# A fourth row buffer and one more unit of lead in a fused attention and gated-layer kernel

## The chip, the cores and the metric

The kernel runs on one core of a Trainium2 chip. The metric is the device time of one execution in microseconds (us); the number given for the kernel before is the median of three runs. Engines are named as in the profile: PE is TensorE (PEld its weight loads), DVE is VectorE, ACT is ScalarE, POOL is GpSimd and SP is SyncE, which does no arithmetic and here issues most of the transfers.

## The reference

Talking-heads attention feeds a gated layer. With batch 4, 12 heads, 448 positions and head size 64, all in float32:

```python
scores = scale * np.matmul(q, k.transpose(0, 1, 3, 2))
scores = np.einsum('bhij,hg->bgij', scores, w_pre)      # first mix over the heads
scores = scores - np.max(scores, axis=-1, keepdims=True)
attn = np.exp(scores)
attn = attn / (np.sum(attn, axis=-1, keepdims=True) + 1e-09)
attn = np.einsum('bhij,hg->bgij', attn, w_post)         # second mix over the heads
attn_out = np.matmul(attn, v)
x = attn_out.transpose(0, 2, 1, 3).reshape(1792, 768)
gate = 1.0 / (1.0 + np.exp(-(x @ w_gate)))
return (gate * (x @ w_val)) @ w_out                     # 768 -> 1536 -> 768
```

## The kernel before

The first 400 us are the attention, the rest is the gated layer, whose matrix products go by a scheme with seven products in place of eight and whose tasks are ordered by a planner with fixed costs. The planner's list is cut at slots of the attention, and neither its costs nor its slots are touched by the change.

**Blocks and units.** Each of the four batches is cut into three blocks of 120 query rows and one of 88. A set is ten query rows with all twelve heads, 120 rows of scores. A unit is two sets; a block of 120 rows has six units, the last block of a batch four and one with a single set, so there are 23 units in a batch and 92 in all. Scores are computed on 128 positions at a time; the eight (or four) left over of each such piece are gathered for the last two units of a batch: the last but one uses a buffer of its own, `T_rest`, the last one, with the single set, an ordinary row buffer, filled by four small transfers.

**The way of a unit.** `scores` (L174) multiplies q with k; `keep` (L182, L185) copies the result from the banks into a stage `st`, half by ACT and half by DVE. `regroup` moves the rows of a unit from the stage into a row buffer `T`, where the 120 partitions are rows and heads, by two transfers on SP's queue (L238; L229 for the rest rows). `premix` (L257) does the first mix on PE from T into three banks `pm`. `rowmax` (L262, DVE), `expo` (L269, ACT), `norm` and `scale` (L274, L275, L281, POOL and DVE) and `p_lo` (L287, DVE) make the normalised weights in two halves; `postmix` (L299) does the second mix on PE, `mix` (L307, ACT) copies it out, and `av` (L326) multiplies a finished block with v. ACT copies that out (L336), and `flush` (L315) stores it through SP's queue.

**The order.** A loop over slots `s` writes the program; slot s has the second mix of unit s. Within it SP first gets the stores that the slot before left (`flush`), then the row transfers of unit s + LEAD (`rows_until`, `regroup`), with LEAD = 5; PE gets the first mix of unit s + 3 (SOFT), then a job of scores, then the second mix of unit s, then `av`. So a unit's rows are requested two slots before the slot of its first mix. The row buffers are used in turn, `t_bufs[u % len(t_bufs)]`: with three of them, the transfer for unit u overwrites what the first mix of unit u - 3 read, in the slot before. A table `plan` gives slots to the score jobs of the next block (from `first[bi - 1] - LEAD` to `first[bi] - LEAD`), to the loads of k (L147), q (L154) and v (L192), and to the early loads of the gated layer's weights (`raws`, L1088); all but the v and the weight loads depend on LEAD. SP takes its instructions in order: a transfer that waits holds all behind it. Before the first unit the loop runs LEAD slots in which only rows, scores and first mixes stand.

Of the kernel before, what the change touches and what calls it, by code (L numbers as in the profile page):

```python
# [9 lines left out]
F32 = mybir.dt.float32  # L10
# [39 lines left out]
def _attention(ctx, tc, ins, B, H, S, D, xs, raws, make_moe):  # L50
# [18 lines left out]
    tp, ep, pp, sm = (grp_ctx.enter_context(tc.tile_pool(name=f"a_{n}", bufs=b))  # L69
                          for n, b in (("t", 1), ("e", 3), ("p", 2), ("s", 4)))  # L70
# [89 lines left out]
    def jobs_of(bi):  # L160
        return NP * blocks[bi][6] // SB
# [48 lines left out]
    nm_t, e_t, ss_t, p_t, mx_t = {}, {}, {}, {}, {}  # L210
    mixes = [mp.tile([128, 4, H, QB], F32, name=f"mix{i}") for i in range(2)]

    t_bufs = [tp.tile([128, 2, S], F32, name=f"T{i}") for i in range(3)]
    t_rest = tp.tile([128, 2, S], F32, name="T_rest")
    for T in t_bufs + [t_rest]:
        nc.gpsimd.memset(T[:64 - HK], 0.0)
# [96 lines left out]
    def flush():  # L313
        while stores:
            nc.sync.dma_start(out=stores[0][0], in_=stores.pop(0)[1])  # L315
# [23 lines left out]
                flush()  # L339


    LEAD = 5
    SOFT = 3
    EARLY_AT = (5, 12, 19, 27, 34, 42, 49, 57)
    BOUND = (0, 6, 10, 11, 12, 13, 14)
# [2 lines left out]
    def at(slot, fn, *args):  # L348
        plan.setdefault(slot, []).append((fn, args))

    def spread(i, n, s0, s1):
        return s0 + i * (s1 - s0) // n

    taken = {EARLY_AT[k] + slot for k in range(moe.EARLY) for slot in (11, 12)}
    for b in range(B):
        f = first[PB * b]
# [13 lines left out]
        for c in range(NP if b else 0):  # L370
            at(spread(c, NP, first[PB * (b - 1)] + 6, first[PB * b - 1] - LEAD - 2), k_load, b, c)
    for bi in range(1, NBK):
        s0, s1 = first[bi - 1] - LEAD, first[bi] - LEAD
        n, skip = jobs_of(bi), 0
        if bi % PB == 0:
            s0, skip = first[bi - 2] - LEAD, jobs_of(bi - 1)
        elif n < NP and bi + 1 < NBK:
            s1 = first[bi + 1] - LEAD
        of = n + skip if skip else n + NP if n < NP and bi + 1 < NBK else n
# [68 lines left out]
    def rows_until(u, done):  # L448
        while done < min(NU, u + 1):
            regroup(done)  # L450
            done += 1
        return done

    next_dma = 0
    for s in range(min(min(plan), -LEAD), max(plan) + 1):
        flush()
        next_dma = rows_until(s + LEAD, next_dma)
        todo = plan.get(s, ())
# [798 lines left out]
@with_exitstack  # L1257
def kernel(ctx, tc, B, H, S, D, ins, out):
    nc = tc.nc
    top = ctx.enter_context(tc.tile_pool(name="top", bufs=1))  # L1260
    dram = ctx.enter_context(tc.tile_pool(name="dram", bufs=1, space=DRAM))
    xs = dram.tile([B, H * D // 128, 128, S], F32, name="xs")
    with tc.manual_schedule():
        raws = top.tile([128, 13 * H * D // 2], F32, name="raws")
        with ExitStack() as c2:
            moe = _attention(c2, tc, ins, B, H, S, D, xs, raws,
                             lambda NG: _Moe(tc, xs, ins, out, raws, NG, top))
        moe.run()
# [72 lines left out]
```

## Time and profile before

| | us |
|---|---|
| median of 3 runs (lowest, highest) | 843.75 (842.42, 844.67) |
| the profiled execution | 844.52 |
| its span | 842.7 |
| PE busy | 793.8 (94%) |
| DVE, ACT, POOL busy | 633.7, 563.7, 280.6 |
| granted PE clock, mean over the span | 0.975 |

The span runs from the first instruction of the profile to the last, and the execution's own time is 1.8 us longer. Busy times are those of instructions in work; a busy PE is not PE at its peak. In the slices of the page PE is at 9 tenths or more almost everywhere after 400 us and between 7 and 9 before; transfers have their densest slices at 6 to 8 tenths in the attention and at 9 late in the gated layer.

### The profile page before, as it was taken

The numbers are of one execution on the slowest core, as the hardware profiler recorded it, in microseconds if no ns is written. First come the engines' busy times: TensorE is split into PE (matmuls) and PEld (weight loads), VectorE is DVE, ScalarE is ACT, GpSimd is POOL, SyncE is SP. The second block draws the span as 40 slices with busy tenths as digits, with TensorE's granted clock in tenths as the row PEclk, the third lists the DMA queues.
The fourth block names the chain that finished last, engine by engine and source line by source line (L and its number), as shares of the span: only waits on it lengthen the run. The fifth ranks groups of instructions, "written<-read, shape, count | busy, mean of one in ns | idle before, by whom it ended". The sixth has DMA issues, their size and how long they took to land.

```text
span 842.7 us, 23449 instructions
## 1 busy us (share of the span) xinstructions
PE 793.8 (94%) x9530; PEld 432.9 (51%) x9530; DVE 633.7 (75%) x1068; ACT 563.7 (67%) x1106; POOL 280.6 (33%) x462
## 2 busy tenths in 40 slices
PE   8989799898989989896999989999999999999998
PEld 2446465464555555465555445555555555555554
DVE  4978587784887778778899799669986999998000
ACT  3888577884878877876777586657874776553100
POOL 1527456474456553342021331223322231110000
PEclk9999899997999999997999999999999999999999
DMA  5686458863786547455653453675546897987001
GB/s 193 214 235 197 149 149 234 260 185 103 227 235 208 163 159 222 156 169 172 218 169 121 151 176 146 229 244 188 174 161 219 313 344 314 340 333 284 34 29 71
DMA packets 80760, 166.13 MB, mean 197 GB/s; under 512 B 20492, under 2 KB 58220, under 8 KB 80652
## 3 DMA queue, kind: packets, MB, share of 16 engines
q1 hardware_dynamic: 72348, 132.83, 50.0%
q0 software_dynamic: 7728, 31.27, 9.4%
q8 instruction: 75, 1.23, 0.6%
q10 hardware_dynamic: 576, 0.53, 0.2%
q14 instruction: 33, 0.27, 0.1%
HBM read 87.75 MB, written 38.15 MB: 149 GB/s over the span
## 4 chain that ended last, share of the span: by engine, by line
PE 71%; DMA 17%; DVE 4%; ACT 4%; issue 1%; POOL 1%; SPq 1%; ACTq 0%; POOLq 0%; DVEq 0%
PE bank L1198 29%; PE bank L1209 17%; DMA T<-st 13%; PE pm L257 9%; PE qk L174 5%; PE av L326 5%; PE mx L299 5%; DMA k<-in_kp_dram 2%; DVE m L1182 1%; DMA v<-in_vb_dram 1%; ACT e L269 1%; DMA m<-w 1%; ACT raws L1129 1%; ACT mix L307 1%; POOL raws L1135 1%
## 5 line engine op out<-in xcount | busy, mean ns | idle before, releaser
L1198 PE MATMUL bank<-m,m 128*128 128x448 f16 x1152 | 221.0, 352 | 4.7 <-ACT m L1218 4.6
L1198 PEld LDWEIGHTS <-m 128*128 128x128 f16 x1512 | 148.0, 98 | 144.4 <-issue 7.5
L281 POOL TENSOR_SCALAR ph<-e,ss 128x448 f16<-128x448 f32 x180 | 112.8, 638 | 177.6 <-DVE ss L275 145.3
L269 ACT ACTIVATE e<-pm,nm 128x448 f32<-128x448 f32 x180 | 114.0, 634 | 82.0 <-DVE nm L262 75.0
L262 DVE TENSOR_REDUCE nm<-pm 128x1 f32<-128x448 f32 x180 | 103.8, 618 | 76.7 <-PE pm L257 75.7
L257 PE MATMUL pm<-T,w 64*64 64x448 f32 (+1 forms) x688 | 131.7, 577 | 28.6 <-DMA T<-st 26.9
L287 DVE SCALAR_TENSOR_TENSOR pl<-e,ss,ph 128x448 f16<-128x448 f32 x180 | 119.9, 706 | 2.0 <-POOL ph L281 2.0
L174 PE MATMUL qk<-k,q 64*64 64x448 f32 x640 | 112.0, 572 | 1.4 <-DMA k<-in_kp_dram 0.8
L1209 PEld LDWEIGHTS <-m 128*128 128x128 f16 x756 | 74.0, 98 | 69.0
L307 ACT ACTIVATE mix<-mx 128x960 f32<-128x960 f32 (+1 forms) x92 | 103.4, 1124 | 2.9 <-PE mx L299 2.6
L299 PEld LDWEIGHTS <-ph 64*128 64x128 f16 x2880 | 65.7, 95 | 75.7 <-issue 40.6
L326 PE MATMUL av<-mix,v 128*64 128x120 f32 (+1 forms) x1504 | 85.3, 268 | 0.0
L299 PE MATMUL mx<-w2hi,ph 64*128 64x60 f16 x1440 | 73.1, 191 | 8.6 <-ACT mix L307 6.4
L1209 PE MATMUL bank<-m,m 128*128 128x448 f16 x396 | 79.3, 352 | 0.0
L1135 POOL CAST raws<-raws 128x768 f16<-128x768 bf16 x36 | 37.8, 1051 | 118.5 <-ACT raws L1129 118.4
L326 PEld LDWEIGHTS av<-mix,v 128*64 128x64 f32 x1504 | 75.2, 140 | 2.6 <-ACT m L1177 0.4
L299 PE MATMUL mx<-w2hi,pl 64*128 64x60 f16 x1440 | 72.1, 190 | 0.4 <-DVE pl L287 0.4
L299 PE MATMUL mx<-w2lo,ph 64*128 64x60 f16 x1440 | 72.2, 190 | 0.0
L1198 PE MATMUL bank<-m 128*128 128x448 f16 x360 | 71.6, 356 | 0.0
L257 PEld LDWEIGHTS pm<-T,w 64*64 64x64 f32 (+1 forms) x688 | 32.4, 134 | 65.8 <-DMA T<-st 23.5
L299 PEld LDWEIGHTS <-pl 64*128 64x128 f16 x1440 | 62.8, 95 | 0.6 <-DVE pl L287 0.6
L1225 DVE TENSOR_TENSOR m<-bank,m 128x448 f32<-128x448 f32 x72 | 44.4, 620 | 23.0 <-PE bank L1198 12.7
(130 smaller groups left out, 1113.5 us busy)
## 6 DMA issues: line engine op xcount, KB each, us to landing
T<-st SPq DMA_DIRECT2D x168, 210.0 KB
m<-w SPq DMA_DIRECT2D x59, 384.0 KB
raws<-in_w_dram SPq DMA_DIRECT2D x28, 767.6 KB
hs<-m POOLq DMA_DIRECT2D x48, 224.0 KB, 4.8
m<-hs SPq DMA_DIRECT2D x15, 672.0 KB
w<-m POOLq DMA_DIRECT2D x21, 384.0 KB, 6.6
w<-raws POOLq DMA_DIRECT2D x20, 384.0 KB, 4.9
v<-in_vb_dram SPq DMA_DIRECT2D x12, 512.0 KB
```

Source lines behind the costliest of these rows:

```text
L174: nc.tensor.matmul(sc[e][64 * half:64 * half + 64, :S], lhsT=q[rows, ch, s0:s0 + 64], rhs=k_t[b, ch][rows, :], start=True, stop=True)
L257: nc.tensor.matmul(pm[bank][64 * x:64 * x + 64, :S], lhsT=w1[rows], rhs=T[rows, x], start=True, stop=True)
L262: nc.vector.tensor_reduce(nm[:, i:i + 1], pm[bank][:, :S], axis=AX.X, op=ALU.max, negate=True)
L269: nc.scalar.activation(out=e_t[u][:, i], in_=pm[units[u][2][i]][:, :S], func=AF.Exp, bias=nm_t[u][:, i:i + 1], scale=1.0, accum_out=ss_t[u ...
L281: nc.gpsimd.tensor_scalar(ph[:, i], e_t[u][:, i], ss_t[u][:, i:i + 1], 1.0, op0=ALU.mult, op1=ALU.mult)
L287: nc.vector.scalar_tensor_tensor(pl[:, i], e_t[u][:, i], ss_t[u][:, i:i + 1], p_t[u][0][:, i], op0=ALU.mult, op1=ALU.subtract)
L299: nc.tensor.matmul(mx[:, x, i, jb * HK:(jb + 1) * HK], lhsT=p[rows, i, JB[jb]:JB[jb] + 128], rhs=w[rows], start=(k == 0), stop=(k == 2))
L307: nc.scalar.activation(out=out.rearrange("p g (y r) -> p y g r", r=HALF), in_=mx_t.pop(u), func=AF.Copy, scale=1.0 / (P_UP * W_UP))
L326: nc.tensor.matmul(av_t[bi][64 * i:64 * i + 64, c % 4, :n], lhsT=vt[b, u][:, h + i, jb, :], rhs=mixes[bi % 2][:, jb, 2 * c + i, :n], start ...
L1135: self.nc.gpsimd.tensor_copy(word.bitcast(F16), word.bitcast(BF16))
L1198: self.nc.tensor.matmul(self.f32(bank), lhsT=w[a][:, k], rhs=x[b][:, k], start=self.START[i] and k == r == 0, stop=k == self.KH - 1 and r ...
L1209: self.nc.tensor.matmul(self.f32(bank), lhsT=w[a][:, k], rhs=b[bb], start=self.START[i] and j == k == r == 0, stop=j == OUT_TILES - 1 and ...
```

## The change

The row buffers go from three to four, and LEAD from 5 to 6. T_rest stays one buffer. Everything that is placed by LEAD moves by one slot: the row transfers, the score jobs, the q loads and the end of the k loads.

```diff
-    t_bufs = [tp.tile([128, 2, S], F32, name=f"T{i}") for i in range(3)]
+    t_bufs = [tp.tile([128, 2, S], F32, name=f"T{i}") for i in range(4)]
     t_rest = tp.tile([128, 2, S], F32, name="T_rest")
     for T in t_bufs + [t_rest]:
         nc.gpsimd.memset(T[:64 - HK], 0.0)
...
-    LEAD = 5
+    LEAD = 6
     SOFT = 3
```

First SP at the end of batch 0, where the last unit's buffer is filled by four pieces (L229); T_170 to T_172 are the three row buffers, raws the gated layer's early weights, xs the attention's output. Before:

```order
L315 DMA xs<-xt 128x4x120
L238 DMA T_172<-st 120x1x448 x2
L1088 DMA raws<-in_w_dram 128x1536
L1088 DMA raws<-in_w_dram 128x1533
L315 DMA xs<-xt 128x2x120
L229 DMA T_171<-st 48x1x448
L229 DMA T_171<-st 12x1x448
L229 DMA T_171<-st 36x1x448
L229 DMA T_171<-st 24x1x448
```

And now, with T_173 as the fourth:

```order
L315 DMA xs<-xt 128x4x120
L1088 DMA raws<-in_w_dram 128x1536
L229 DMA T_172<-st 48x1x448
L229 DMA T_172<-st 12x1x448
L229 DMA T_172<-st 36x1x448
L229 DMA T_172<-st 24x1x448
L1088 DMA raws<-in_w_dram 128x1533
L315 DMA xs<-xt 128x2x120
L238 DMA T_173<-st 120x1x448 x2
```

The four pieces moved ahead of the second weight load and of the second store, with the unit before them gone from between.

Then SP in the second block of batch 0, where the v, k and q of the next batch are loaded. Before:

```order
L192 DMA v<-in_vb_dram 128x1024
L147 DMA k<-in_kp_dram 128x448 x2
L1088 DMA raws<-in_w_dram 128x1536
L238 DMA T_170<-st 120x1x448 x2
L147 DMA k<-in_kp_dram 128x448
L154 DMA q<-in_qp_dram 128x768
L1088 DMA raws<-in_w_dram 128x1536
L238 DMA T_171<-st 120x1x448 x2
L147 DMA k<-in_kp_dram 128x448
```

And now:

```order
L238 DMA T_170<-st 120x1x448 x2
L192 DMA v<-in_vb_dram 128x1024
L147 DMA k<-in_kp_dram 128x448 x2
L154 DMA q<-in_qp_dram 128x768
L1088 DMA raws<-in_w_dram 128x1536
L238 DMA T_171<-st 120x1x448 x2
L147 DMA k<-in_kp_dram 128x448
L1088 DMA raws<-in_w_dram 128x1536
L238 DMA T_172<-st 120x1x448 x2
L147 DMA k<-in_kp_dram 128x448 x2
```

The rows in T_170 are those of the same unit in both, and now stand ahead of the v and k loads; the q load has moved up by a slot, and two of the later k loads stand together.

Last PE at the start, where T_170 is the first unit's buffer and qk the banks of a score job of the second block (four matmuls). Before:

```order
L174 MATMUL qk<-k,q 64x448 x8
L257 MATMUL pm_115<-T_170,w_118 64x448
L257 MATMUL pm_116<-T_170,w_118 64x448
L257 MATMUL pm_115<-T_170,w_118 64x448
L257 MATMUL pm_116<-T_170,w_118 64x448
```

And now:

```order
L174 MATMUL qk<-k,q 64x448 x12
L257 MATMUL pm_115<-T_170,w_118 64x448
L257 MATMUL pm_116<-T_170,w_118 64x448
L257 MATMUL pm_115<-T_170,w_118 64x448
L257 MATMUL pm_116<-T_170,w_118 64x448
```

Three score jobs in place of two stand ahead of the first first mix.

## Rows read from the trace of the kernel before

**Rows 1.** The page's part 4: the chain that ended last, by engine, by line.
```profile
PE 71%; DMA 17%; DVE 4%; ACT 4%; issue 1%; POOL 1%; SPq 1%; ACTq 0%; POOLq 0%; DVEq 0%
PE bank L1198 29%; PE bank L1209 17%; DMA T<-st 13%; PE pm L257 9%; PE qk L174 5%; PE av L326 5%; PE mx L299 5%; DMA k<-in_kp_dram 2%; DVE m L1182 1%; DMA v<-in_vb_dram 1%; ACT e L269 1%; DMA m<-w 1%; ACT raws L1129 1%; ACT mix L307 1%; POOL raws L1135 1%
```
**Rows 2.** Windows: stretch, length, busy us of PE, PEld, DVE, ACT, POOL, clock, transfers.
```profile
0.00:400.00 400.00, 359.54 (x7168) 207.48 (x7169) 299.34 (x610) 298.97 (x669) 192.45 (x328) 0.95 0.64 191
400.00:842.70 442.70, 434.27 (x2363) 225.39 (x2361) 334.33 (x458) 264.73 (x438) 88.16 (x134) 1.00 0.57 203
```
**Rows 3.** Waits of PE: engine, line, releaser: us in total, times, longest.
```profile
PE pm L257 <- DMA T<-st: 26.9, 22, 4.2
PE mx L299 <- ACT mix L307: 6.4, 6, 2.5
```
**Rows 4.** Timeline of PE, last units: start, us, what, [idle before <-releaser].
```profile
100.00 0.97 PE L257 MATMUL pm<-T,w 64*64 64x448 f32 x1 [4.16 <-DMA T<-st]
...
198.30 0.98 PE L257 MATMUL pm<-T,w 64*64 64x448 f32 x1 [3.77 <-DMA T<-st]
...
297.19 0.56 PE L257 MATMUL pm<-T,w 64*64 64x448 f32 x1 [2.37 <-DMA T<-st]
...
383.17 0.56 PE L257 MATMUL pm<-T,w 64*64 64x448 f32 x1 [2.11 <-DMA T<-st]
```
**Rows 5.** Windows by block, each between two copies L307, columns as in rows 2.
```profile
43.25:70.45 27.20, 24.38 (x480) 14.12 (x474) 19.65 (x39) 22.31 (x52) 9.82 (x19) 0.94 0.84 227
...
91.65:116.55 24.90, 20.74 (x376) 11.75 (x372) 13.50 (x27) 14.16 (x32) 13.09 (x20) 0.79 0.45 144
...
140.40:168.30 27.90, 24.70 (x484) 13.94 (x476) 20.48 (x41) 22.08 (x52) 13.39 (x22) 1.00 0.83 250
...
190.35:215.30 24.95, 21.18 (x378) 12.20 (x372) 13.95 (x29) 13.89 (x30) 10.88 (x18) 0.79 0.42 129
215.30:240.30 25.00, 22.50 (x500) 12.84 (x497) 20.31 (x49) 18.64 (x44) 13.96 (x23) 1.00 0.80 228
240.30:267.75 27.45, 24.67 (x480) 14.12 (x475) 20.86 (x43) 22.12 (x52) 13.91 (x23) 0.94 0.76 233
...
290.65:310.15 19.50, 17.13 (x378) 10.69 (x372) 13.89 (x28) 13.38 (x30) 11.73 (x18) 1.00 0.46 151
310.15:333.80 23.65, 22.72 (x498) 12.99 (x496) 18.73 (x41) 18.69 (x44) 9.20 (x19) 1.00 0.66 197
...
377.55:397.20 19.65, 12.62 (x296) 10.32 (x297) 15.60 (x24) 15.07 (x23) 5.70 (x10) 0.76 0.62 187
```
**Rows 6.** Timeline of SP, 88 to 101.5 us: issues of transfers, start, us.
```profile
88.35 0.38 SPq L315 DMA_DIRECT2D xs<-xt  x1
88.83 4.21 SPq L229 DMA_DIRECT2D T<-st  x4
```
**Rows 7.** Windows around the wait that ends at 100 us, columns as in rows 2.
```profile
97.70:99.95 2.25, 0.00 (x0) 0.00 (x0) 0.00 (x0) 0.00 (x0) 1.34 (x2) 0.50 0.32 98
99.95:107.90 7.95, 7.91 (x86) 3.07 (x88) 3.76 (x8) 3.23 (x7) 2.22 (x4) 0.50 0.59 201
```
**Rows 8.** The chain in order of time, 36 to 70 us: start, us, what.
```profile
36.30 7.82 DMA v<-in_vb_dram
...
44.13 8.42 DMA k<-in_kp_dram
...
52.62 8.72 DMA T<-st
```
**Rows 9.** The page's part 6: transfers by line, count, KB each.
```profile
T<-st SPq DMA_DIRECT2D x168, 210.0 KB
```
**Rows 10.** The chain in order of time, 10 to 18 us: score jobs.
```profile
12.74 0.98 PE qk L174 x8
...
14.29 1.71 PE qk L174 x8
```
**Rows 11.** Groups of POOL in the first 5 us: busy us, mean ns of one.
```profile
L216 POOL MEMSET T<- 4x896 f32 x3 | 2.4, 834 | 0.3 <-POOLq L1327 0.3
```

## The prediction

> **What bounds the kernel now.** I read the share of the chain that ended last first: TensorE (PE) makes up 71% of it and transfers 17%, and one transfer group alone, the gather of score rows into the row buffers (T<-st), is 13%, some 113 us of a span of 842.7 [rows 1]. Then the busy time by stretch: PE works 359.54 us of the first 400, the attention, and 434.27 of the other 442.7, the gated layer [rows 2]. So the second part is nearly full of matmuls, its instructions stay in their order, and what can be won lies in the 40 idle us of the attention. Third, PE's own waits: 26.9 us in 22 waits before the first mix (L257) end with the landing of a T transfer; the next kind, for the copy of mixed scores, is 6.4 us [rows 3]. Fourth, where these waits lie: four of them, the longest of each batch, are 4.16, 3.77, 2.37 and 2.11 us, 12.4 together [rows 4]; each stands before the batch's last unit, the one with a single set. The other 14.5 us lie mostly in the second block of a batch. Fifth, the cost of each block of six units (five in a batch's last block), cut from one copy L307 to the sixth after it [rows 5]. A second block takes 27.20, 27.90 and 27.45 us in batches 0 to 2, while a first block without an idle wait for T took 23.65. A last block takes 24.90 and 24.95 us in batches 0 and 1, but 19.50 in batch 2.
>
> Why the last unit waits is in SyncE's timeline [rows 6]: the four small pieces of its buffer are issued from 88.83 on, right after the store of the attention rows at 88.35, and the issue ends at 93.04; PE goes on at 100.00, 6.96 us later. In that wait PE does nothing, the granted clock is 0.50 (1.2 GHz of 2.4), and it stays there for the next 8 us in which PE is busy nearly all the time [rows 7].
>
> **The change part by part.** Every row transfer stands one unit earlier in SyncE's queue, and the buffer that it writes was read by the first mix of four units before, which itself is one unit earlier in the program; so the transfer waits for that no longer than now, and has three units' time to land in place of two. The scores of a block, their q loads and the last k load of a batch move with it.
>
> *The last units.* In the order, their pieces now stand ahead of one weight load and of the store that held them. The lead grows by one unit, 17.1/5 = 3.4 us (17.1 is the third such block, 19.50, without its wait of 2.37), against waits of 4.16 and 3.77: at most 0.8 us is left. The whole block then falls from 24.90 and 24.95 towards 17.1 us, because with a wait of 2.37 its granted clock was 1.00 and with the two longer ones 0.79 [rows 5]: upper end 7.8 + 7.85 + 2.4 = 18.0 us. Lower end: the waits shrink only to that of the third block, 5.4 + 5.45 = 10.8. I take 16, each wait but the 0.8 us gone, since nothing in the order still stands between the scores and these pieces. The fourth such wait, 2.11 us, lies among the first loads of the gated layer (clock 0.76, transfers 0.62); 0 to 2.1, I take 1.
>
> *The second blocks.* Upper end: 27.20, 27.90 and 27.45 each fall to 23.65, which is 3.55 + 4.25 + 3.8 = 11.6 us. Lower end 0: transfers fill 0.84, 0.83 and 0.76 of the 16 engines there [rows 5], and the chain in 36 to 70 us is one transfer waiting for another, a v load of 7.82 us, a k load of 8.42, a row transfer of 8.72 [rows 8]. Where the transfers are the limit, an earlier issue buys only what is queued behind it now and was ahead of it before, the other loads of one unit. In the block from 140.40 us, 250 GB/s for 27.90 us are 6.97 MB, of which the rows are 12 transfers of 210 KB [rows 9], 2.58 MB; the rest, 4.39 MB, is 0.73 MB or 2.9 us per unit. But a q load and a k load come one unit earlier in just these blocks, and the row transfers behind them pay for that. Between 0 and 2.9 us a block I take 1.5, so 4.5.
>
> *The other blocks* lose little: the first of batch 2 takes 25.00 us, 1.35 above the undisturbed one, with PE idle for 2.5 of them [rows 5]. 0 to 2.5, I take 1.
>
> *The start.* Three score jobs in place of two now stand ahead of the first first mix. A job follows the other after 14.29 - 12.74 = 1.55 us, and both are on the chain [rows 10]; the job is missing later, where its matmuls alone would have cost 0.98 us. 0 to 1.55 us lost, I take 1.55 - 0.98 = 0.6. The fourth buffer's fill on GpSimd is 0.834 us [rows 11]; GpSimd has nothing else until the first row transfer lands, over 10 us later. Were that cover gone it would cost its 0.8.
>
> No wait is added. What becomes late next, once T is there: VectorE and ScalarE are busy 13.5 and 14.2 us of the 24.90, and 18.7 of the undisturbed 23.65, so they have room; the copy of mixed scores (6.4 us of waits) stays.
>
> Sum: 16 + 1 + 4.5 + 1 - 0.6 = 21.9 us. The profiled execution took 844.5 us, the median of the runs is 843.75: 822.6 against the first, 822 against the second. All terms at their upper ends give 18.0 + 2.1 + 11.6 + 2.5 = 34.2, so 809.5 on the median's scale; all at the lower 10.8 - 1.55 = 9.3, so 834.5.
>
> A rule that speaks against it: the Trainium skill, "DMA: Bandwidth & Descriptors", section "Why a DMA increments its semaphore by 16 and not by 1", says that a transfer is split over the largest number of engines up to 16 that divides the slowest dimension of both sides; the row transfers read 10 partitions and write 120, so they would run on ten engines. Taking time by bytes, those ten would then be full in the second blocks (an estimate from that page and rows 5: 37% of 0.83 on ten is 0.49, with the other 0.52 it is 1.0), and the sum without the second blocks would be 17.4. No row here tells the engines apart.
>
> **The rivals.**
> *Transfers set the pace.* The bound moves from "issued late" to "moved slowly": second blocks stay at 27 to 28 us and the last units keep a wait like that of batch 2. For it: 0.83 busy transfers and the chain of transfers [rows 5, 8]. Against: at a batch's end transfers are at only 0.45, and there the larger part is to be won. Gain 10.8 - 0.6 = 10.2, so about 833.5. The rule above is on this rival's side.
> *No change.* Each wait for T is taken over by another, for the copy of mixed scores or a bank that ScalarE still reads. For it: 6.4 us of such waits already. Against: batch 2's last block took 19.50 with the same work as those of 24.9. About 843.5.
> *Slower.* The k loads' first use comes one unit earlier, while the first two are issued in the same unit as before. From the end of that unit it is now two units, 2 x 23.65/6 = 7.9 us, against 8.42 us from issue to landing in rows 8. PE's order is fixed, so all later mixes stand behind these scores. If k lands w later than that, PE idles w at three places, one per batch, and a wait of some 4 us cost about as much again in half clock (24.95 - 19.50 less the 1.4 us by which the waits differ is 4.0). At w = 5 it is 3 x 9 = 27 us lost against 16 won at the last units, so about 855. It decides where 3w, or 3 x (w + 4) with the clock, passes the 16: between w = 1.3 and 5.3, a load of 9 to 13 us. Against: the 8.42 us were taken in the block with the highest share of all, 0.84.
> *Does not do what it says:* SyncE is behind anyhow, so that a place earlier in its order is no time earlier. That holds where it waits for landings, and is the first rival's second-block part.
>
> **How the numbers follow.** Forecast (815 to 828) 0.50, a larger gain (809 to 815) 0.10, transfers set the pace (828 to 838) 0.25, no change 0.08, slower 0.07. A measurement here can tell 0.3%, 2.5 us, from no change. Faster is 0.50 + 0.10 + 0.25 = 0.85, the same 0.08, slower 0.07. The range 811 to 838 leaves out 0.15 above and a few hundredths below; the forecast's own is 815 to 828.
>
> **What would show it.** Waits of PE for T from 26.9 to under 8 us, those of the last units under 1; the granted clock 0.95 or more in each batch's last block, and its time 17 to 19 us; second blocks at about 26; the chain's share of T<-st from 13% to under 6%; from the end of the attention on the same 443 us. It is wrong if last blocks still take over 22 us, if PE's waits for k appear in L174, or if the second part grows by what the first loses.

## The result and the profile after

The changed kernel takes 815.4 us (median of six runs, 810.22 to 820.93) against 843.26 for the kernel before beside it (six runs, 839.80 to 846.09): a ratio of 0.9667 [0.9621, 0.9712], 27.9 us less. Forecast were 822 and a range of 811 to 838. The profiled execution took 812.46 us, its span is 810.6, and the granted clock has a mean of 0.987 where it had 0.975.

The page's part 4 of the changed kernel, the chain that ended last by engine and by line, answers to [rows 1]:

```profile
PE 72%; DMA 10%; DVE 6%; ACT 5%; issue 4%; POOL 2%; SPq 0%; ACTq 0%; POOLq 0%; DVEq 0%
PE bank L1198 27%; PE bank L1209 18%; PE pm L257 9%; DMA T<-st 7%; PE av L326 6%; PE qk L174 6%; PE mx L299 6%; DMA q<-in_qp_dram 2%; DVE m L1182 2%; POOL raws L1135 1%; DVE pl L287 1%; DVE nm L262 1%; ACT e L269 1%; ACT raws L1129 1%; ACT mix L307 1%
```

The row transfers go from 13% of the chain to 7%, and a new transfer is on it, the q load with 2%. The waits of PE after (engine, line, releaser: total us, times, longest) answer to [rows 3]:

```profile
PE mx L299 <- ACT mix L307: 10.6, 9, 4.3
PE qk L174 <- DMA q<-in_qp_dram: 5.6, 2, 2.9
...
PE pm L257 <- DMA T<-st: 2.8, 5, 0.9
...
PE qk L174 <- DMA k<-in_kp_dram: 1.1, 1, 1.1
```

T has fallen from 26.9 us in 22 waits to 2.8 in 5, none over 0.9. Two lines have grown by more than 4 us: the copy of mixed scores from 6.4 to 10.6, and q from nothing to 5.6. The one wait for k lies at the start, where 0.8 us of it stood before too. The two parts of the span after, as windows (stretch, length, busy us of PE, PEld, DVE, ACT, POOL, clock, transfers), answer to [rows 2], and the blocks below them to [rows 5]. The attention's last copy ends at 367.5 us:

```profile
0.00:375.00 375.00, 345.44 (x7285) 205.78 (x7286) 305.14 (x615) 304.98 (x680) 197.93 (x329) 0.98 0.67 204
375.00:810.60 435.60, 427.35 (x2247) 220.03 (x2245) 328.88 (x454) 257.31 (x427) 89.80 (x134) 1.00 0.57 205
42.96:67.32 24.36, 21.42 (x467) 12.32 (x460) 19.14 (x39) 21.62 (x51) 10.16 (x20) 1.00 0.86 247
89.14:106.15 17.01, 16.48 (x372) 10.52 (x370) 14.66 (x28) 13.54 (x33) 13.46 (x20) 1.00 0.73 234
127.75:154.63 26.88, 22.04 (x472) 12.61 (x467) 20.84 (x42) 21.77 (x52) 14.49 (x24) 1.00 0.84 251
178.00:195.47 17.47, 17.47 (x374) 10.81 (x372) 14.34 (x32) 13.27 (x31) 12.43 (x19) 1.00 0.64 198
217.13:244.01 26.88, 23.09 (x473) 13.94 (x470) 20.44 (x43) 21.87 (x52) 14.83 (x24) 0.94 0.84 253
284.04:304.81 20.77, 20.77 (x502) 12.60 (x498) 18.62 (x42) 18.64 (x45) 9.73 (x19) 1.00 0.72 223
344.52:367.45 22.93, 14.05 (x321) 12.12 (x321) 16.55 (x24) 15.34 (x25) 5.70 (x10) 0.78 0.69 209
```

The sixteen blocks of the two kernels, cut alike (us; four blocks a batch, the first with the start):

| batch | before | after | difference |
|---|---|---|---|
| 0 | 43.2, 27.2, 21.2, 24.9 | 43.0, 24.4, 21.8, 17.0 | -0.2, -2.8, +0.6, -7.9 |
| 1 | 23.8, 27.9, 22.1, 24.9 | 21.6, 26.9, 23.4, 17.5 | -2.2, -1.0, +1.3, -7.4 |
| 2 | 25.0, 27.5, 22.9, 19.5 | 21.7, 26.9, 23.4, 16.7 | -3.3, -0.6, +0.5, -2.8 |
| 3 | 23.6, 24.1, 19.7, 19.7 | 20.8, 20.7, 19.0, 22.9 | -2.8, -3.4, -0.7, +3.2 |

Nearly all of the gain lies in the attention: its last copy ends at 367.5 instead of 397.1 us, and from there to the end of the span it is 443.1 us where it was 445.6. The last blocks of batches 0 to 2 give 18.1 us at a clock of 1.00, the second blocks 4.4, and 12.4 come from the first blocks of batches 1 to 3 and from the second and third of batch 3. Lost again are 2.4 in the third blocks and 3.2 in the very last one.

Why the last unit of a batch no longer waits is in SP's timeline after (start, us, issued transfers), which answers to [rows 6]:

```profile
81.43 5.06 SPq L229 DMA_DIRECT2D T<-st  x4
86.53 1.66 SPq L1088 DMA_DIRECT2D raws<-in_w_dram  x1
88.30 1.58 SPq L315 DMA_DIRECT2D xs<-xt  x1
```

The four pieces are issued by 86.49, ahead of the weight load and of the store that held them, and the first mix that reads them follows 5.45 us later with no wait, as PE's timeline shows:

```profile
91.94 0.59 PE L257 MATMUL pm<-T,w 64*64 64x448 f32 x2
```

### The profile page after: what moved, and what is told of

Same layout as the page of the kernel before. It is cut to its first block, busy times and chain, and to the rows that moved or that the text cites. A ratio compares the mean times of both kernels' runs of the same rounds, so it can differ in the third digit from the quotient of the medians.

```text
span 810.6 us, 23451 instructions
## 1 busy us (share of the span) xinstructions
PE 772.8 (95%) x9530; PEld 425.8 (53%) x9530; DVE 634.0 (78%) x1068; ACT 562.3 (69%) x1106; POOL 287.7 (35%) x463
## 4 chain that ended last, share of the span: by engine, by line
PE 72%; DMA 10%; DVE 6%; ACT 5%; issue 4%; POOL 2%; SPq 0%; ACTq 0%; POOLq 0%; DVEq 0%
PE bank L1198 27%; PE bank L1209 18%; PE pm L257 9%; DMA T<-st 7%; PE av L326 6%; PE qk L174 6%; PE mx L299 6%; DMA q<-in_qp_dram 2%; DVE m L1182 2%; POOL raws L1135 1%; DVE pl L287 1%; DVE nm L262 1%; ACT e L269 1%; ACT raws L1129 1%; ACT mix L307 1%
## 5 line engine op out<-in xcount | busy, mean ns | idle before, releaser
L287 DVE SCALAR_TENSOR_TENSOR pl<-e,ss,ph 128x448 f16<-128x448 f32 x180 | 121.7, 716 | 2.1 <-POOL ph L281 2.0
L257 PE MATMUL pm<-T,w 64*64 64x448 f32 (+1 forms) x688 | 115.1, 567 | 6.3 <-ACT e L269 3.2
L174 PE MATMUL qk<-k,q 64*64 64x448 f32 x640 | 96.1, 548 | 9.9 <-DMA q<-in_qp_dram 5.6
L307 ACT ACTIVATE mix<-mx 128x960 f32<-128x960 f32 (+1 forms) x92 | 103.5, 1125 | 2.3 <-PE mx L299 2.0
L299 PE MATMUL mx<-w2hi,ph 64*128 64x60 f16 x1440 | 72.6, 190 | 11.1 <-ACT mix L307 10.6
L1129 ACT ACTIVATE raws<-raws 128x768 int16<-128x768 int8 (+1 forms) x56 | 50.7, 905 | 12.7 <-POOL raws L1135 12.6
```

Source lines behind the costliest of these rows:

```text
L174: nc.tensor.matmul(sc[e][64 * half:64 * half + 64, :S], lhsT=q[rows, ch, s0:s0 + 64], rhs=k_t[b, ch][rows, :], start=True, stop=True)
L257: nc.tensor.matmul(pm[bank][64 * x:64 * x + 64, :S], lhsT=w1[rows], rhs=T[rows, x], start=True, stop=True)
L287: nc.vector.scalar_tensor_tensor(pl[:, i], e_t[u][:, i], ss_t[u][:, i:i + 1], p_t[u][0][:, i], op0=ALU.mult, op1=ALU.subtract)
L299: nc.tensor.matmul(mx[:, x, i, jb * HK:(jb + 1) * HK], lhsT=p[rows, i, JB[jb]:JB[jb] + 128], rhs=w[rows], start=(k == 0), stop=(k == 2))
L307: nc.scalar.activation(out=out.rearrange("p g (y r) -> p y g r", r=HALF), in_=mx_t.pop(u), func=AF.Copy, scale=1.0 / (P_UP * W_UP))
L1129: self.nc.scalar.activation(out=out, in_=src, func=AF.Copy, scale=by)
```

## The experiments

The theory after the result: the unit of lead alone makes the gain, because T is requested a unit earlier and past what stood ahead of it; in the second blocks the transfers are the limit. Rivals were that the fourth buffer itself does it, that the gain at the last units is only the clock, and that in the second blocks the late q, not the sum of the transfers, holds PE. The block times of an experiment are those of one profiled execution; how far two executions of the same kernel differ is shown at the end.

### One part alone

The fourth buffer alone, with the lead of before:

```diff
-    t_bufs = [tp.tile([128, 2, S], F32, name=f"T{i}") for i in range(3)]
+    t_bufs = [tp.tile([128, 2, S], F32, name=f"T{i}") for i in range(4)]
     LEAD = 5
```

> Four row buffers, lead still five units. Theory (the place in SyncE's queue counts, the buffer only makes it possible): the transfers stand where they stood, only the wait for the buffer's earlier reader goes; the chain shows hardly any of that, so 842 us, within 2.5 of before, and PE's waits for T still 24 to 28 us. Rival (the transfers were held by the buffer): 825 or less, waits for T under 12 us.

843.71 us, ratio 1.0001 [0.9976, 1.0026]. The waits of PE, and then the last block of batch 0 (windows):

```profile
PE pm L257 <- DMA T<-st: 29.5, 22, 4.3
```
```profile
91.11:116.23 25.12, 20.85 (x375) 11.86 (x370) 13.47 (x27) 14.15 (x32) 13.13 (x20) 0.80 0.45 143
```

29.5 us of T waits for 26.9, and 25.12 us for 24.90: a buffer more, with nothing requested earlier, changes nothing.

The lead of six with three buffers. The request for unit s + 6 then overwrites what the first mix of unit s + 3 has just read, so it has to be written behind that mix; the two lines that ask for the very last rows a slot ahead go:

```diff
-    LEAD = 5
+    LEAD = 6
...
-        next_dma = rows_until(s + LEAD, next_dma)
...
         rowmax(s + SOFT)
+        next_dma = rows_until(s + LEAD, next_dma)
...
-        if s >= NU - LEAD - 3:
-            next_dma = rows_until(s + 1 + LEAD, next_dma)
```

> Three row buffers, but the rows of unit s + 6 are requested in slot s behind the first mix of unit s + 3, which frees their buffer; scores, q and k are placed as with a lead of six. The rule that requests two units in each of the last slots is left out. Theory (lead counts): PE's first mix stands at the front of a slot, so nearly the whole unit of lead is there without a fourth buffer: 816 to 822 us, waits for T under 8 us. Rival (the buffer is needed, since SyncE now stands still until PE has done that mix and holds the loads behind it): 832 to 843 us, waits for T 12 us or more.

811.71 us, ratio 0.9621 [0.9574, 0.9669]. Waits of PE, and the last block of batch 0:

```profile
PE pm L257 <- DMA T<-st: 6.5, 8, 2.5
```
```profile
90.51:108.14 17.63, 16.85 (x371) 10.84 (x370) 14.64 (x29) 13.54 (x33) 13.47 (x20) 1.00 0.74 229
```

That is less time than was expected (816 to 822). The whole gain is there without the fourth buffer; its interval and the changed kernel's overlap. The lead is the cause, and the buffer one way to allow it. The fair partner of this version is the kernel with four buffers that leaves out the same two lines (809.46 us, below): 2.3 us less, and a second such pair below differs by 2.6 the same way. So the buffer may add some 2 us, which these intervals cannot tell from nothing.

Only the four pieces of each batch's last unit a unit earlier, all else at the lead of five (four buffers):

```diff
-        while done < min(NU, u + 1):
+        while done < min(NU, u + 1 + (u + 1 < NU and len(units[u + 1][1]) == 1)):
```

> Four buffers, lead five, only the rows of each batch's last unit (the four small pieces) are requested one slot earlier. Theory: the last blocks of batches 0 and 1 fall from 24.9 to about 17 us and that of batch 2 from 19.5 to about 17, together 16 to 18 us, the second blocks stay at 27 to 28; the last batch's pieces now stand ahead of the gated layer's first weight loads, as with the whole change, and may lose 3 us. 826 to 830 us. Rival (the pieces are held by the transfers, not by their place): under 8 us won, 836 or more.

829.11 us, ratio 0.9817 [0.9764, 0.9870]. The last blocks of batches 0, 1 and 3:

```profile
90.35:108.98 18.63, 17.95 (x375) 10.72 (x370) 13.83 (x27) 13.56 (x32) 12.89 (x20) 1.00 0.65 204
183.16:200.37 17.21, 17.15 (x377) 10.62 (x372) 14.08 (x30) 13.28 (x31) 11.81 (x18) 1.00 0.57 182
362.55:384.45 21.90, 12.87 (x302) 11.28 (x304) 16.01 (x24) 15.34 (x24) 5.73 (x10) 0.72 0.69 216
```

6.3 and 7.7 us less, with the third 3.0 less, and 2.2 more in batch 3: 14.8 us by the blocks, 15.4 by the medians (the kernel before took 844.53 beside it). That is half of the whole change, by itself, and the loss at the end of batch 3 comes with it. The first blocks of batches 1 to 3 stay at 23.8, 26.4 and 24.2 us.

### What the half clock cost

Twenty idle matmuls on zeros are put in front of the first mix of the last units of batches 0 and 1, so that PE works through the wait; the wait itself stays:

```diff
+    fill = tp.tile([128, 512], F16, name="fill")
+    nc.vector.memset(fill, 0.0)
...
+        if u in (22, 45):
+            for _ in range(20):
+                nc.tensor.matmul(pm[banks[0]], lhsT=fill[:, :128], rhs=fill, start=True, stop=True)
```

> The kernel before, with 20 matmuls of 128 x 512 zeros on PE just ahead of the first mix of the last unit of batches 0 and 1, into the bank that this mix then overwrites; nothing else is moved. PE then waits as long for T, but not idle. Theory (of the 7.8 us that each of these blocks lost, about 4 are the half clock after the wait): clock 1.00 in both blocks, each falls from 24.9 to about 21, the kernel to 834 to 837 us. Rival (the other engines bind there, the half clock costs nothing): blocks stay at 24 to 25, 842 to 846 us.

838.67 us, ratio 0.9928 [0.9897, 0.9959]: faster beyond the noise, but by less than was expected. The two blocks:

```profile
89.96:111.73 21.77, 21.77 (x394) 12.67 (x390) 13.68 (x27) 13.67 (x32) 12.92 (x20) 1.00 0.52 164
186.74:207.36 20.62, 20.62 (x397) 12.33 (x392) 14.00 (x30) 13.37 (x31) 11.60 (x18) 1.00 0.50 149
```

With the clock kept at 1.00 (2.4 GHz), 3.1 and 4.3 us of the 7.9 and 7.5 go; the rest, 4.8 and 3.2 us, is left for the wait itself. So the waits of 4.16 and 3.77 us cost 3.1 and 4.3 us more in half clock, as the prediction had put it for the rival of the k loads (4.0).

### What holds the second blocks

Batches 1 to 3 use the k of batch 0, so that 18 k loads of 224 KB fall away:

```diff
     def k_load(b, c):
+        if b:
+            k_t[b, c] = k_t[0, c]
+            return
```

> The changed kernel without the k loads of batches 1 to 3 (all batches use the k of batch 0, so the scores of batches 1 to 3 are of the wrong keys): 18 loads of 224 KB less, just in the second blocks, nothing else moved. Theory (there the transfers set the pace, now as before): second blocks of batches 0 to 2 fall from 24.4, 26.9 and 26.9 us to 21 to 22.5, PE's waits for q in them go, 800 to 805 us. Rival (the order of the engines' own work sets these blocks): they stay above 24.5, 811 to 816 us.

805.2 us, ratio 0.954 [0.9491, 0.9588]. The three second blocks:

```profile
43.98:65.56 21.58, 21.11 (x472) 12.55 (x472) 18.93 (x39) 21.38 (x51) 10.10 (x19) 1.00 0.74 223
126.57:150.00 23.43, 21.85 (x477) 12.56 (x474) 20.17 (x41) 21.55 (x51) 14.07 (x23) 1.00 0.74 230
212.16:235.53 23.37, 22.26 (x481) 13.37 (x484) 20.92 (x42) 21.45 (x52) 14.61 (x23) 1.00 0.74 231
```

2.8, 3.5 and 3.5 us less than in the changed kernel, with transfers at 0.74 in place of 0.84 to 0.86, and 0.9 us of waits for q in place of 5.6. Two of the blocks stay above the 22.5 us expected. Against a second execution of the changed kernel (21.6, 25.8 and 26.3 us, see the end) it is 0.0, 2.3 and 2.9 us less. So in batches 1 and 2 what is moved there sets the pace; for batch 0 it is not shown. The loads that are gone have left SP's queue as well, so this run does not tell their bytes from their places in the queue.

The rival, that it is the q load's place: q one slot earlier.

```diff
-            at(slots[0] - (3 if skip else 4), q_load, bi)
+            at(slots[0] - 4, q_load, bi)
```

> The changed kernel with the q load of each next batch's first block one slot earlier (four slots ahead of its first score job, as the other blocks' q loads are, not three), and so ahead of the v and k loads of the second block. Theory (q is the new late transfer, 5.6 us of PE waits in batches 1 and 2, with a short half clock after each): 806 to 811 us, waits for q gone. Rival (the second blocks are full of transfers, another one is late in its place): 813 to 817 us, waits for k or T of some 5 us more.

812.69 us, ratio 0.9625 [0.9585, 0.9665], between the two expectations and not to be told from the changed kernel. Its waits of PE have no line for q any more, but:

```profile
PE pm L257 <- DMA T<-st: 7.9, 10, 1.9
```

5.6 us of q waits have gone, 5.1 us of T waits have come (3.5 and 3.9 against the second execution). Second blocks take 24.8, 26.4 and 25.9, third ones 23.6, 23.8 and 24.9. A transfer put ahead makes another late.

Half of the row transfers of the second blocks left away (one set per unit in place of two), 18 transfers of 210 KB:

```diff
-            for x in range(2):
+            for x in range(1 if j == 1 and bi < 12 else 2):
```

> The changed kernel, but in the second blocks of batches 0 to 2 only the first of a unit's two row transfers is made (18 transfers of 210 KB left out, 3.9 MB; the second half of those units is mixed from an older unit's rows). Without the k loads, 18 of 224 KB or 4.1 MB, the kernel was at 805.2. Theory (a row byte in these blocks costs what a k byte does): the same gain for the same bytes, 9 to 10 us, 803 to 806 us. Rival (rows are moved on ten of the sixteen engines, as the rule weighed in the prediction has it, and those ten are the full ones): a row byte costs 1.6 times a k byte, until the blocks are at the 20.7 us of batch 3's, 798 to 802 us. If the rows are no part of the pace: 810 or more.

809.19 us, ratio 0.959 [0.9554, 0.9626]. The first two second blocks:

```profile
43.66:65.27 21.61, 21.15 (x472) 12.53 (x472) 18.95 (x39) 21.40 (x51) 10.07 (x19) 1.00 0.83 263
125.66:152.13 26.47, 21.78 (x467) 12.57 (x468) 20.71 (x42) 21.75 (x51) 15.24 (x24) 1.00 0.81 234
```

The third takes 24.4. Neither the theory nor the rival forecast this time. 3.9 MB less of rows gain 5.6 us in these blocks (4 to 6 by the medians), where 4.1 MB less of k gained 9.7 (8 to 10). A byte of rows is not dearer here than a byte of k. Whether it is cheaper the runs cannot tell: the intervals of the two ratios overlap, and in batch 0 the second execution of the changed kernel took 21.6 us as well.

The k loads moved to quieter blocks: those of batch 1 from the middle of batch 0 to its start, those of batches 2 and 3 to the last block of the batch two before (together with the edit of the next section, and once more in the version with three buffers):

```diff
-                at(spread(c, NP, first[PB * (b - 1)] + 6, first[PB * b - 1] - LEAD - 2), k_load, b, c)
+                s0 = first[PB * (b - 1) - 1] if b > 1 else 0
+                at(spread(c, NP, s0, s0 + 5), k_load, b, c)
```

> The changed kernel, with the last unit's rows behind the weights at the end, and with the k loads moved out of the second blocks: those of batches 2 and 3 into the last block of the batch two before (transfers there at 0.45), those of batch 1 into its first slots. The same bytes. Theory (second blocks are full of transfers, and places with room exist): second blocks of batches 1 and 2 from 26.9 to 23 to 24.5 us, the last blocks of batches 0 and 1 stay at 17 to 18.5, 800 to 806 us. Rival (the loads cost as much wherever they stand): 808 to 813 us.

> As the run before in its k loads, but with three row buffers and the rows requested behind the first mix. If the fourth buffer adds nothing: within 3 us of the run before, 800 to 807 us. If, with the k loads out of the way, the second blocks gain from the buffer: 4 us or more slower than the run before.

814.5 us, ratio 0.964 [0.9602, 0.9678], and with three buffers 817.14, ratio 0.9673 [0.9638, 0.9708]. The second blocks of batches 0 and 1, and the first and second of batch 2, with four buffers:

```profile
44.48:72.01 27.53, 24.06 (x485) 13.33 (x488) 19.15 (x39) 22.00 (x52) 10.15 (x19) 1.00 0.76 219
132.75:156.67 23.92, 22.90 (x481) 13.51 (x484) 20.01 (x41) 21.44 (x51) 13.16 (x22) 1.00 0.77 241
199.24:224.56 25.32, 22.56 (x494) 12.47 (x494) 20.02 (x47) 18.67 (x44) 14.07 (x23) 1.00 0.84 239
224.56:248.75 24.19, 22.24 (x481) 12.76 (x478) 20.47 (x43) 21.77 (x51) 14.43 (x24) 1.00 0.72 234
```

The second blocks of batches 1 and 2, which have lost their k loads, are 3.0 and 2.7 us shorter, as the theory had it (with three buffers 23.6 and 24.4 us). But that of batch 0, behind the loads that now stand at the start, is 3.2 us longer, and the first block of batch 2, behind those of batch 3, 3.6 longer; with three buffers they take 28.1 and 25.5. The total is no lower, against 800 to 806 expected: the loss has moved with the loads. Not every place pays: the first block of batch 1, behind the loads of batch 2, takes 22.2 us, against 21.6 and 22.3 in the two executions of the changed kernel.

### The end of the attention

The last block of batch 3 is the one that lost. Here SP's timeline after shows the order that the change made, the last pieces ahead of the gated layer's first weights (m<-w):

```profile
337.11 5.33 SPq L229 DMA_DIRECT2D T<-st  x4
342.49 4.21 SPq L1150 DMA_DIRECT2D m<-w  x4
```

ACT has the conversion of these weights in its order ahead of the attention's last work, and PE waits behind it. That it is the weights' landing which ACT awaits, the row does not name (its releaser is "issue"); the rows of ACT and of PE after:

```profile
348.22 1.12 ACT L1177 ACTIVATE m<-m,one_w 128x384 f16<-128x384 f32 x2 [3.13 <-issue]
```
```profile
352.52 0.23 PE L299 MATMUL mx<-w2hi,ph 64*128 64x60 f16 x2 [4.34 <-ACT mix L307]
```

The experiment leaves out the two lines by which the last rows are asked for a slot ahead, so that the weights come first again:

```diff
-        if s >= NU - LEAD - 3:
-            next_dma = rows_until(s + 1 + LEAD, next_dma)
```

> The changed kernel without the rule that requests two units in each of the last slots, so that the rows of the last unit stand behind three of the gated layer's first weight loads, as in the kernel before. Theory (the last block lost 3.3 us because these loads fell behind the rows, and ScalarE stands still for them): last block from 22.9 to 19 to 20.5 us, 811 to 813 us. Rival (PE then waits for the last unit's rows as long): last block 22 or more, 814 to 817 us.

809.46 us, ratio 0.9591 [0.9545, 0.9637]. SP's timeline, and the block:

```profile
341.42 3.05 SPq L1148 DMA_DIRECT2D m<-w  x3
344.57 5.17 SPq L229 DMA_DIRECT2D T<-st  x4
```
```profile
348.81:369.11 20.30, 12.64 (x308) 10.08 (x310) 15.41 (x24) 15.02 (x23) 5.72 (x10) 0.83 0.61 183
```

20.30 us in place of 22.93: three of the four weight loads stand first, and the loss is gone but for 0.6. ACT no longer stands idle ahead of the conversion; PE waits 2.9 us for the last rows instead. The size is not as sure as the sign. The versions that leave out these two lines have this block at 20.3, 20.3, 21.6, 22.0 and 19.8 us, those that keep them, with a lead of six, at 22.9, 22.5, 22.2, 21.3 and 23.1. This version's 809.46 us is the lowest median of a kernel that leaves no work out, but its interval overlaps that of the changed kernel, and the profiled execution was the longest of the six (815.53).

With q a slot earlier as well:

> The changed kernel with both of the edits before. If they add up: 803 to 808 us. If the second blocks or the end take back what is won: 810 to 815.

812.69 us, ratio 0.9622 [0.9578, 0.9667]: the last block has its 20.3, and the rest gives nothing on top. And the changed kernel once more, with no edit, beside these:

> The changed kernel once more, unaltered, on the chip of the two runs that follow, so that they can be set against it: 812 to 818 us.

813.27 us, ratio 0.9627 [0.9593, 0.9660]. Single blocks differ by up to 2.8 us between two profiled executions of it (its first second block takes 21.6 here, 24.4 above). So the blocks of one execution show a mechanism only where the difference is larger or comes again in several blocks, and this holds for every experiment above. The 2.8 us that the runs with one k and with half the rows gained in batch 0 are therefore not theirs for sure: all three executions have 21.6 us there.

## Why the prediction was right, and where it was not

**As a whole**, 21.9 us were forecast and 27.9 measured by the medians; 815.4 lies at the lower edge of the forecast's own 815 to 828, and the second measurement of the changed kernel, 813.27, just below it. The largest term was right in its mechanism. Two terms missed in opposite directions, the other blocks by some 9 us too little and the fourth last unit by 4 too much, so the sum came out better than its parts.

**The last units** were forecast at 16 us (10.8 to 18.0) and gave 18.1 in batches 0 to 2, its upper end. The step "at most 0.8 us is left" was too careful: nothing was left, since the issue of the four pieces ends 5.45 us before they are read. That the block falls towards 17.1 us, the wait and the half clock both, held to 0.4 (17.0, 17.5, 16.7), and the filler splits the gain of a long wait in the wait's part and the clock's, 3 to 5 us each. The lead alone does it, shown by the version with three buffers and by the one that moves these pieces only.

**The fourth last unit** was put at a gain of 1 and lost 3.2 (2.8 in the second execution). The prediction saw that it lies among the first loads of the gated layer, but not that its pieces would now pass three of these loads and that ACT, in whose order their conversion stands ahead of the last mixes, waits there (that it waits for these weights is argued from the order, not shown by a row). With the weights first again, 2.6 of the 3.2 come back in two versions, 1.0 to 3.2 over all five.

**The second blocks** were forecast at 4.5 and gave 4.4, though not 1.5 each: 2.8, 1.0 and 0.6, and in the second execution 5.6, 2.1 and 1.2, together 8.9. That the sum came so near is luck. That transfers set the pace in those of batches 1 and 2 is shown: without the k loads they are shorter, with q earlier T is late instead, and with the k loads elsewhere they are shorter but other blocks longer. But the prediction had the row transfers pay for the q and k loads, and it is the q load that came too late: PE waits 5.6 us for it, and hardly for T. Its step "No wait is added" failed here; the waits for q are new, and those for the copy of mixed scores grew by 4.2 us. So the first rival's mechanism is real in these blocks, and its other half, that the last units would keep a wait, is not.

**The ten engines.** The Trainium skill, "DMA: Bandwidth & Descriptors", section "Why a DMA increments its semaphore by 16 and not by 1", would have the row transfers on ten engines, each byte of them 1.6 times as dear to the fullest engines as a byte of k on sixteen (an estimate from that page). Measured per MB, rows left out gave 5.6 / 3.9 = 1.4 us and k 9.7 / 4.1 = 2.4; against the second execution of the changed kernel (second blocks 21.6, 25.8, 26.3) the gains are 1.2 and 5.3 us, in the same order. The price by that rule is not borne out here; how the transfers were split no row shows.

**The other blocks** are the term that was mis-sized: 1 us forecast, 2.5 at most, and about 10 measured (12.4 gained, 2.4 lost in third blocks). It failed at its yardstick: the "undisturbed" block of 23.65 us [rows 5] was itself held by T. PE was idle in it for 0.93 us, a wait for T that the prediction passed over. More of the waiting is not under PE at all. In the first mix T is the moving operand and the weights are the mixing matrix, yet the trace has waits for T ahead of the weight loads, listed under PEld. The waits of PEld in that block of the kernel before, 310.15 to 333.80 (PE's 0.93 us are the end of the longest), and from the chain of that block its longest piece:

```profile
PEld pm L257 <- DMA T<-st: 2.9, 3, 1.7
```
```profile
315.00 8.27 DMA T<-st
```

23.65 less these 2.9 is the 20.8 of the same block after, whose chain is PE's work alone. In the timeline of PE before, such a wait looks like work:

```profile
316.56 1.66 PE L257 MATMUL pm<-T,w 64*64 64x448 f32 x6
317.64 0.59 PE L174 MATMUL qk<-k,q 64*64 64x448 f32 x2
318.05 0.54 PE L257 MATMUL pm<-T,w 64*64 64x448 f32 x2
```

The eight matmuls recorded for one unit's first mix are split into six and two, with score matmuls between them, over 2.0 us in place of 1; the same place in PEld's timeline shows what held them:

```profile
317.62 0.14 PEld L257 LDWEIGHTS pm<-T,w 64*64 64x64 f32 x2 [0.73 <-DMA T<-st]
```

Over the whole span PEld's waits for T were 23.5 us in 33 before; after they are

```profile
PEld pm L257 <- DMA T<-st: 9.6, 16, 1.0
```

Some of these lie beside other work, and none may be added to PE's own. In the first blocks of batches 1 to 3 they were 3.2, 2.9 and 2.9 us before and 0.8, 0.8 and nothing after, and these blocks gained 2.2, 3.3 and 2.8. Where only the last units' pieces were moved, 2.0, 2.1 and 2.2 us of them stay, and so do the blocks' times (23.8, 26.4 and 24.2). So these 8.3 us come from the rest of the change, the lead of the other units. The 3.4 us of batch 3's second block are not explained by it: PE waited 0.7 us for T there and PEld 0.6. What gave them is open.

**The start** was put at a loss of 0.6 and gained 0.2, which the runs cannot tell from nothing. **No change** and **Slower** fell: the only wait for k, 1.1 us, lies at the start, so k was not late at any of the three places named. Of the signs named ahead, four held (T waits under 8, none of the last units' over 1, second blocks at about 26, and 443 us from the end of the attention, though that was 445.6 before). The rest failed: batch 3's last block had a clock of 0.78 and took 22.9 us, past the 22 named as a sign of being wrong, and the chain's share of T is 7%, not under 6%.

## What to carry to other kernels

A wait for a matmul's input can stand ahead of its weight load, even where the input is not the weights; so the waits are to be read under the weight loads as well as under the matmuls, and a block counts as undisturbed only when neither waits. In this kernel a request moved a place ahead gained what it passed where transfers left room (0.45 in the last blocks); where they were the limit (0.84) it chose which one was late, and only leaving loads out helped. Ahead of a move, the other customers of the queue are to be looked through at each place of the program, the ends of loops above all: three of four ends gained, and the fourth lost; by the order of ACT's work, what was passed there was needed at once.

## What the hardware showed beyond that

The clock did not follow the length of the wait alone. Stretches of the changed kernel, as windows: behind a wait of 2.69 us for q (to 142.71), behind one of 1.96 us for the exponentials (to 153.72), behind one of 2.95 us for q (to 232.13), and behind the 4.34 us at the end.

```profile
142.70:150.70 8.00, 8.00 (x160) 4.45 (x160) 4.93 (x10) 6.23 (x15) 4.41 (x7) 1.00 0.92 280
154.58:158.00 3.42, 3.36 (x18) 0.85 (x18) 1.16 (x2) 1.95 (x7) 2.10 (x4) 0.50 0.62 215
233.09:236.50 3.41, 3.41 (x61) 2.23 (x62) 1.89 (x4) 2.57 (x5) 1.24 (x2) 0.50 1.05 294
352.56:362.80 10.24, 7.20 (x174) 6.76 (x175) 9.05 (x14) 7.42 (x11) 3.38 (x6) 0.50 0.73 227
```

After 2.69 us the clock stayed at 1.00 (2.4 GHz); after 1.96, 2.95 and 4.34 us it was 0.50 (1.2 GHz) in the stretches shown, longest by far after the last. What decides between the first three is open.

The issue of the four small pieces took SP 4.21, 5.31, 4.35 and 4.69 us at the four ends before, and 5.06, 4.73 and 5.33 us at three of them after. It has no fixed price here, and the share of busy transfers while it runs does not order it: it took 5.31 us at 0.44 and 4.69 at 0.72.
